# Second spectral piece behind the first W piece, gate_w row ahead of w_down, w_up in nine loads

## The chip, the cores and the metric

One NeuronCore of a Trainium2 chip runs the whole program. The metric is the device time of one execution in microseconds (us), lower is better. The profile is one execution, so a stage is read from it and a difference of a few us in the total is read from the timed runs.

## The reference, cut to what matters

Forward and all gradients of a gated mix of a spectral filter and a gated feed-forward block:

```python
g = sigmoid((x * gate_w).sum(-1, keepdims=True))     # x: 2048 x 576
a = irfft2(rfft2(x) * (w_r + 1j * w_i))              # spectral branch
b = (gelu(x @ w_gate) * (x @ w_up)) @ w_down         # w_gate, w_up: 576 x 4608
out = g * a + (1 - g) * b                            # returned with 7 gradients
```

## The kernel before: the parts that matter

Phase one walks 18 groups of the hidden dimension, each in four steps of 512 rows. A step on TensorE is: 16 z matmuls and four small ones, the xy matmuls in two halves, then "jobs" (weight-gradient work, here W: pieces of 16 matmuls of 1.75 us, and dwd pieces of 8 of 0.98 us), with a few spectral pieces between them. The scheduling is by program order, engine by engine.

```python
z, xy_full = H_mm(g, m)                   # TensorE; z is in pool pz, one buffer
...
second()                                  # second xy half, its q, xb, hu copies on ScalarE
jobs = carry + hs                         # (weight, function) pairs: W and dwd pieces
us = sum(j[0] for j in jobs)
at, k, late = 0.0, 0, [sigs]
for w, f in jobs:
    if k < n and at >= k * us / n:        # n spectral pieces, evenly spaced
        fft_next(); k += 1                # matmuls to pz (TensorE), copy out (ScalarE)
    f()                                   # W or dwd matmuls; every second one ends in a ScalarE copy
    at += w
    if late and at >= 2.5:
        late.pop()()                      # sigs: two sigmoids (ScalarE), then 8 VectorE operations
while k < n:
    fft_next(); k += 1
```

A spectral piece writes `pftile()`, which from the second group on is always the one buffer of `pz` that z uses too. So TensorE may start a piece, or the next z, only when the last piece has been copied out. The pieces come in three stretches: forward (f1, f2: lines L549, L566), middle (s2, s1: L659, L748) and inverse (Z, ZU, d: L794, L806, L820/L822).

Phase two reads the stored activations back, transposed (`pin`, six buffers), and multiplies them with `wgT`, `wd_all`, `wuT` in jobs called g, b, u.

```python
ensure()                                  # first six pin loads; all loads are in one queue (SP)
for f0 in range(0, NFC, FCB):
    LD.dma_start(wd_all[:, f0:f0 + FCB, :], ...)          # w_down, 5.2 MB in three
... # the last W pieces of phase one
gwr = p2res.tile([1, D], BF16, name="gwr")                # memory that phase one used
LD.dma_start(gwr[:], gate_w.rearrange("(o d) -> o d", o=1))
... # for job i: one w_up load of 6 blocks if i > 1; spread_gw() (needs gwr) at i == 1
```

## Time and profile before

| | us |
|---|---|
| median of the first 3 runs (range) | 1506.61 (1506.12 to 1510.05) |
| span of the profiled run | 1507.8 |
| TensorE busy | 1396.5 |
| ScalarE busy | 721.8 |
| VectorE busy | 731.7 |

With TensorE busy 93% of the span, only its idle time and its time at a lowered clock can be won. The lines that show where it waits are in the prediction below.

For comparing kernels I cut each span at the first matmul of certain steps (start times in the TensorE timeline, subtracted): "head" to the start of the second group; "forward" to step 11; "middle" to step 46; "inverse" to step 65 (steps counted from 0, four a group); "last steps" to phase two; "to first b" job; "b jobs" to the first u job; "rest".

| kernel | head | forward | middle | inverse | last steps | to first b | b jobs | rest |
|---|---|---|---|---|---|---|---|---|
| before | 92.9 | 105.0 | 463.0 | 289.5 | 111.8 | 33.8 | 75.2 | 336.6 |

### The profile page before, as it was taken

How to read it: one execution, taken by the hardware profiler on the slowest of the kernel's cores; microseconds unless marked ns; L12 is line 12 of the kernel's file. 1: busy time of each engine (PE TensorE's matmuls, PEld its weight loads, DVE VectorE, ACT ScalarE, POOL GpSimd, SP SyncE). 2: the span in 40 equal slices, each digit the busy share in tenths (PEclk: the TensorE clock that was granted, in tenths of full speed). 3: DMA queues.
4: the chain of work that ended last, by engine and by line, in shares of the span. 5: the costliest groups of instructions: out<-in, count | busy, mean ns of one | idle time of the engine just before them, and what ended most of it. 6: DMA issues, size and time to landing. Idle time of an engine off the chain costs nothing.

```text
span 1507.8 us, 28114 instructions
## 1 busy us (share of the span) xinstructions
PE 1396.5 (93%) x11342; PEld 1028.9 (68%) x11414; DVE 731.7 (49%) x1394; ACT 721.8 (48%) x1311; POOL 125.7 (8%) x230
## 2 busy tenths in 40 slices
PE   6888899999999999999998999999998999999997
PEld 4556566666666666766666666678676777777775
DVE  6674456777766776755555554553000461222110
ACT  5776677777777776666566666663000000000000
POOL 3000010011001001100101000000000110000000
PEclk9999999999999999999999999999999999999999
DMA  5333354544564453453444454576999998877773
GB/s 188 95 101 112 98 139 117 152 111 133 147 156 119 128 157 99 121 148 99 123 138 113 129 150 124 138 166 142 224 186 197 207 217 158 168 160 162 157 151 70
DMA packets 516381, 214.96 MB, mean 143 GB/s; under 512 B 312825, under 2 KB 510458, under 8 KB 516250
## 3 DMA queue, kind: packets, MB, share of 16 engines
q1 hardware_dynamic: 506618, 192.64, 54.7%
q0 software_dynamic: 7824, 19.49, 4.2%
q8 instruction: 89, 1.46, 0.4%
q10 hardware_dynamic: 1808, 1.02, 0.2%
q14 instruction: 42, 0.34, 0.1%
HBM read 40.76 MB, written 93.84 MB: 89 GB/s over the span
## 4 chain that ended last, share of the span: by engine, by line
PE 81%; ACT 10%; issue 3%; DVE 2%; DMA 2%; POOL 0%; ACTq 0%; DVEq 0%; POOLq 0%
PE acc L1094 27%; PE xy L392 16%; PE wps L495 15%; PE z L380 9%; PE wps L478 7%; ACT om L433 3%; PE xy L387 2%; PE z L383 2%; ACT dw L456 1%; ACT s L434 1%; PE wps L508 1%; DMA pin<-scr 1%; DMA gwr<-in_gate_w_dram 1%; ACT Xg L664 1%; ACT ZT L797 1%
## 5 line engine op out<-in xcount | busy, mean ns | idle before, releaser
L1094 PEld LDWEIGHTS <-pin 128*128 128x128 bf16 x3456 | 339.0, 98 | 92.0 <-DMA pin<-scr 5.0
L392 PE MATMUL xy<-wgu,xT 128*128 128x512 bf16 x1080 | 247.8, 379 | 10.2 <-issue 9.5
L495 PEld LDWEIGHTS <-xn 128*128 128x128 bf16 x2304 | 224.4, 98 | 29.2 <-issue 0.2
L392 PEld LDWEIGHTS <-xT 128*128 128x128 bf16 x1152 | 106.9, 98 | 149.3 <-issue 31.2
L380 PE MATMUL z<-wdT,dOT 128*128 128x256 bf16 x1152 | 145.7, 282 | 33.6 <-ACT Xg L664 14.2
L402 ACT ACTIVATE da<-z,omg 128x256 bf16<-128x256 f32 x288 | 113.0, 475 | 125.5 <-PE z L383 125.5
L1111 ACT COPY bo<-acc 128x288 f32<-128x288 f32 x32 | 12.8, 399 | 316.5 <-PE acc L1094 291.8
L380 PEld LDWEIGHTS <-dOT 128*128 128x128 bf16 x1152 | 115.8, 101 | 57.7 <-issue 40.4
L438 DVE TENSOR_TENSOR xb<-xb,s 128x1024 bf16<-128x1024 bf16 x72 | 49.8, 692 | 211.1 <-ACT s L434 211.1
L478 PE MATMUL wps<-dB,A 128*128 128x288 bf16 x1152 | 151.1, 286 | 0.0
L1094 PE MATMUL acc<-wd_all,pin 128*128 128x288 bf16 x1152 | 143.1, 286 | 4.1 <-DMA pin<-scr 4.1
L1094 PE MATMUL acc<-wgT,pin 128*128 128x288 bf16 x1152 | 146.6, 289 | 0.0
L1094 PE MATMUL acc<-wuT,pin 128*128 128x288 bf16 x1152 | 143.6, 286 | 0.0
L495 PE MATMUL wps<-dHu,xn 128*128 128x256 bf16 x1152 | 132.7, 272 | 0.0
L495 PE MATMUL wps<-dHg,xn 128*128 128x256 bf16 x1152 | 132.5, 273 | 0.0
L478 PEld LDWEIGHTS <-A 128*128 128x128 bf16 x1152 | 112.0, 98 | 28.3
L409 ACT ACTIVATE q<-xy 128x512 bf16<-128x512 f32 x144 | 86.1, 598 | 61.4 <-PE xy L392 61.4
L501 POOL DMA_DIRECT2D out_dram<-dw x67 | 48.8, 728 | 606.3 <-ACT dw L456 594.7
L1171 DVE SCALAR_TENSOR_TENSOR f32t<-gwf,dlog,b16t 128x576 f32<-128x576 f32 x16 | 13.1, 818 | 173.5 <-DMA b16t<-dxa_scr 173.5
L417 DVE TENSOR_SCALAR s<-q 128x1024 bf16<-128x1024 bf16 x72 | 30.7, 426 | 136.3 <-ACT q L409 136.3
L456 ACT CAST dw<-wps 128x512 bf16<-128x512 f32 x72 | 42.2, 586 | 93.5 <-PE wps L495 93.5
L412 ACT CAST hu<-xy 128x512 bf16<-128x512 f32 x144 | 86.9, 603 | 0.0
(197 smaller groups left out, 1637.5 us busy)
## 6 DMA issues: line engine op xcount, KB each, us to landing
scr<-A SPq DMA_DIRECT2D x72, 256.0 KB, 2.6
scr<-dHg SPq DMA_DIRECT2D x72, 256.0 KB, 2.9
scr<-dHu SPq DMA_DIRECT2D x72, 256.0 KB, 3.4
out_dram<-dw POOLq DMA_DIRECT2D x67, 128.0 KB, 2.2
wd_all<-in_B_w_down_dram SPq DMA_DIRECT2D x3, 1728.0 KB, 14.6
out_dram<-dwd POOLq DMA_DIRECT2D x34, 144.0 KB, 3.2
scr_p<-Vt SPq DMA_DIRECT2D x32, 145.0 KB, 3.0
wgu<-in_B_w_gate_dram SPq DMA_DIRECT2D x18, 256.0 KB, 3.3
```

The source lines that it names most:

```text
L380: nc.tensor.matmul(zo(t), lhsT=dOT[:, ci, t, :], rhs=wdT[:, ci, :], start=(t % 4 < 2 and ci == 0), stop=False)
L392: nc.tensor.matmul(xy[k][:, t % 2, :], lhsT=xT[:, ci, t, :], rhs=wgu[:, ci, :], start=False, stop=(ci == 3))
L402: nc.scalar.activation(da[:, t, :], z[:, t % 2, t // 2, :], ACT.Copy, scale=omg32[:, 4 * m + t:4 * m + t + 1])
L409: nc.scalar.activation(q[:, h, :], xy[:, :, 0:FG], ACT.Square)
L412: nc.scalar.copy(hu[:, h, :], xy[:, :, FG:2 * FG])
L433: nc.scalar.activation(om[:], s[:], ACT.Sigmoid, scale=-2.0 * C_GELU)
L438: V.tensor_tensor(xb[:], xb[:], s[:], op=ALU.mult)
L456: nc.scalar.copy(out, in_)
L478: nc.tensor.matmul(wps[:, :288], lhsT=tl(0, t)[:, fch * P:(fch + 1) * P], rhs=dB[:, t, h * 288:(h + 1) * 288], start=(t == 0), stop=(t == ...
L495: nc.tensor.matmul(wps[:, cc, :], lhsT=xn[:, t, (c0 + cc) * P:(c0 + cc + 1) * P], rhs=tl(k, t), start=(t == 0), stop=(t == T - 1))
L501: wst[0].dma_start(ov[:, c0:c0 + TPB, fsl], dw[:])
L1094: nc.tensor.matmul(acc[:, :288], lhsT=src[:, r, :], rhs=w_of(r)[:, h * 288:(h + 1) * 288], start=(first and r == 0), stop=(last and r == F ...
```

## The change

Its intent: the copy of a step's second spectral piece should no longer wait behind the sigmoids and a W copy on ScalarE, the gate_w row should not wait behind w_down, and w_up should load in smaller pieces spread over more jobs.

```diff
-                jobs = carry + hs
-                us = sum(j[0] for j in jobs)
                 at, k, late = 0.0, 0, [sigs]
-                for w, f in jobs:
-                    if k < n and at >= k * us / n:
+                for w, f in carry + hs:
+                    if k < n and at >= (0.0, 1.0, 3.6, 5.0)[k]:
                         fft_next()
                         k += 1
+                    if late and at >= 1.6 and k >= min(n, 2):
+                        late.pop()()
                     f()
                     at += w
-                    if late and at >= 2.5:
-                        late.pop()()
...
     wd_all = p2r.tile([P, NFC, D], BF16, name="wd_all")
+    gwr = p2r.tile([1, D], BF16, name="gwr")
+    LD.dma_start(gwr[:], gate_w.rearrange("(o d) -> o d", o=1))
...
-        LD.dma_start_transpose(wuT[k][:, r0:r0 + 6, :], B_w_up[:, f0 * P:(f0 + 6) * P])
+        LD.dma_start_transpose(wuT[k][:, r0:r0 + 4, :], B_w_up[:, f0 * P:(f0 + 4) * P])
...
-        wT_loads = [(k, r0) for k in range(NB) for r0 in (0, 6)]
+        wT_loads = [(k, r0) for k in range(NB) for r0 in (0, 4, 8)]
...
-        gwr = p2res.tile([1, D], BF16, name="gwr")
-        LD.dma_start(gwr[:], gate_w.rearrange("(o d) -> o d", o=1))
...
-            if i > 1 and wT_loads:
+            if i > 0 and wT_loads:
```

The first hunk holds two effects: the **place** of the second piece (behind one W or dwd piece, not at an even share of the work) and the **order** on ScalarE (sigmoids behind the second copy).

## The prediction

> **What bounds the kernel now.** I read the page first (busy shares, then the chain that ended last), then who waited for whom on TensorE stage by stage, then the timelines of single steps, last the windows for the granted clock.
>
> ```profile
> PE 1396.5 (93%) x11342; PEld 1028.9 (68%) x11414; DVE 731.7 (49%) x1394; ACT 721.8 (48%) x1311; POOL 125.7 (8%) x230
> ...
> PE 81%; ACT 10%; issue 3%; DVE 2%; DMA 2%; POOL 0%; ACTq 0%; DVEq 0%; POOLq 0%
> ```
>
> TensorE (PE) is the bound: 111 us of the 1507.8 us span are idle, and only those, and time at a lowered clock, can be won while its work stays the same. The order view of both kernels has 22830 TensorE instructions in each, so no matmul is removed. The waits of 195 to 680 us, then of 680 to 960 us:
>
> ```profile
> PE z L380 <- ACT Xg L664: 14.2, 8, 1.8
> PE z L380 <- ACT Vt L751: 9.7, 8, 1.2
> ...
> PE pf L820 <- ACT ZT L797: 7.0, 7, 2.2
> PE pf L794 <- ACT ev L826: 6.5, 5, 1.8
> PE pf L820 <- ACT ZU L809: 4.9, 3, 1.9
> PE pf L806 <- ACT ev L826: 3.5, 2, 1.8
> ```
>
> Columns: who waits, for what, us in total, times, longest. Every line is TensorE waiting for a ScalarE (ACT) copy of a spectral piece. The piece (pf) and the next step's z share one PSUM buffer, so nothing goes into it until the previous piece is copied out. Two stretches of ScalarE show why the copy is late or not:
>
> ```profile
> 405.69 1.28 ACT L664 CAST Xx<-pf 64x578 bf16<-64x578 f32 x2
> 407.86 0.59 ACT L456 CAST dw<-wps 128x512 bf16<-128x512 f32 x1 [0.88 <-PE wps L495]
> 408.34 1.06 ACT L433 ACTIVATE om<-s 128x1024 bf16<-128x1024 bf16 x1
> 409.43 1.06 ACT L434 ACTIVATE s<-s 128x1024 bf16<-128x1024 bf16 x1
> 410.39 1.27 ACT L664 CAST Xg<-pf 64x578 bf16<-64x578 f32 x2
> ...
> 432.96 0.85 ACT L751 CAST Vt<-pf 128x580 bf16<-128x580 f32 x1
> ```
>
> The second piece's copy (410.39) stands behind the W copy and two sigmoids, 2.5 us of work, and the next z waits 1.78 us for it. Phase two (from 1062 us):
>
> ```profile
> 1062.21 8.98 PE L1094 MATMUL acc<-wgT,pin 128*128 128x288 bf16 x72
> 1074.91 0.63 PE L1085 MATMUL acc<-gwr,onesr 1*128 1x288 bf16 x2 [3.71 <-DMA gwr<-in_gate_w_dram]
> 1075.47 20.65 PE L1094 MATMUL acc<-wgT,pin 128*128 128x288 bf16 x144
> 1095.96 35.44 PE L1094 MATMUL acc<-wd_all,pin 128*128 128x288 bf16 x288
> 1132.42 8.99 PE L1094 MATMUL acc<-wd_all,pin 128*128 128x288 bf16 x72 [1.01 <-DMA pin<-scr]
> 1143.25 8.99 PE L1094 MATMUL acc<-wd_all,pin 128*128 128x288 bf16 x72 [1.84 <-DMA pin<-scr]
> 1153.52 6.67 PE L1094 MATMUL acc<-wd_all,pin 128*128 128x288 bf16 x53 [1.28 <-DMA pin<-scr]
> ```
>
> A 1.1 KB row, queued behind 5.2 MB of w_down, costs 3.71 us; then 144 matmuls take 20.65 us where 288 take 35.44, so 17.7 at full pace; then three waits for transposed input sum to 4.1 us. The slow 144 have their reason in the windows, whose third-last column is the granted clock:
>
> ```profile
> 1076.00:1078.00 2.00, 2.00 (x10) 1.29 (x9) 0.16 (x1) 0.00 (x0) 0.00 (x0) 0.50 1.14 208
> 1082.00:1084.00 2.00, 2.00 (x19) 1.60 (x17) 0.00 (x0) 0.00 (x0) 0.00 (x0) 1.00 0.54 106
> ```
>
> **What the Trainium skill says.** "TensorE: Matmul & The Clock Gate", part 1 on the clock gate: after about one idle window of 3.4 us the array falls to half clock, and a busy window restores it; the window is free-running. The trace agrees in kind: 0.50 above, and half pace for some 3.4 us at 138, 155, 733, 795, 886 and 917 us, each after waits of 1.8 to 3 us. Here less idle than a full window is enough, and other waits of 1.8 us bring none, which suits a free-running window. The same page, on architectural detail: ScalarE and VectorE are strict FIFOs. The trace agrees: the copy at 410.39 starts as the second sigmoid drains, though its matmuls ended at 408.07. "DMA: Bandwidth & Descriptors", on latency and other measured facts, has 261 GB/s for a DMA transpose with a non-contiguous middle dimension. Here the stretch 1100 to 1150 us moves 164 to 204 GB/s at full DMA share, and that measurement is what I use.
>
> **The change, part by part.** Part one: in each of the 68 steps after the first group, a second piece now follows the first W half (16 matmuls, 1.75 us, or 8 dwd matmuls, 0.98 us), and its copy precedes the sigmoids. This removes the wait at the end of a step, but puts the second piece so close that TensorE waits for the first piece's copy. That copy cannot start before the q, xb, hu copies of the second xy half. Readiness after the last xy matmul, from the trace: for s2 pieces (L659) 3.1 us (matmuls to 403.91, copies to 406.97); for s1 (L748) 2.5 us (431.32 to 433.81; 2.4 in a shorter case); for Z 2.55, of which 0.37 is already seen as a wait at 788.50; for d 2.2; for ZU 1.9. TensorE's cover is the first piece (s1 and s2 0.25, Z 0.45, d 0.5, ZU 0.1) plus 1.75 or 0.98. So the new wait is 1.1 for s2 and 0.55 for s1 ahead of a W half; 1.9 and 1.15 ahead of a dwd half; 0.37, 0, 0 for Z, d, ZU ahead of W, and 1.1, 0.7, 0.8 ahead of dwd.
>
> Middle stretch (195 to 680 us). The order view gives 15 steps with s2 before W, 9 with s1 before W, 1 with s2 before dwd, 6 with s1 before dwd: 15 x 1.1 + 9 x 0.55 + 1.9 + 6 x 1.15 = 30.3 us new. Removed: 14.2 + 9.7 + 0.4 = 24.3. Loss 6.0 us.
>
> Inverse stretch (680 to 960 us, 19 steps with two to four pieces). Removed: 7.0 + 6.5 + 4.9 + 3.5 + 1.8 (ev, L820) + 1.0 (z for ZU) = 24.7. New, step by step: first-piece waits sum to 5.5 (5 Z before W at 0.37, then dwd steps 0.7, 0.7, 0.8, 1.1, and small remains); six steps now have their last piece directly ahead of z and wait for its whole copy (d and ZU about 0.8 each, Z 1.2 each), 5.5 together; third pieces waiting for a copy behind sigmoids and W copy, about 0.8. Sum 11.8, gain 12.9. No wait is over 1.3 us, so I expect the four half-clock spells here (733, 795, 886, 917) to go, all but about half of one: 3.5 x 3.4 us x 0.5 = 6 us.
>
> Forward stretch (123 to 211 us, six steps). Removed 11.4 (two waits of 3.0, 2.0, 1.8 and small ones). New 9.7: 0.5 and 0.6; then 3.4 and 2.4 where a third piece still sits behind the sigmoids; 1.5 and 1.4 around the table pieces. Gain 1.7. Its two half-clock spells stay.
>
> Part two, the gate_w row: ahead of all input loads it lands long before 1071 us; the ones row it multiplies is set at 1069.8, also in time. From 1071.2 to 1096.0 us TensorE would need 0.3 + 17.7 = 18.0 us instead of 24.8: gain 6.8, of which 3.7 is wait and about 3 clock.
>
> Part three, nine w_up loads of four blocks from the second job on, in place of six of six. Before, a job asks for three inputs (1.18 MB) and 0.88 MB of w_up in 8.85 us, 233 GB/s, more than the 164 to 204 moved. After, 1.18 + 0.59 MB, 200 GB/s, about what the queue does, and it starts where DMA is half idle (shares 0.46 to 0.83 at 1082 to 1090). With six input buffers ahead, nearly all of 4.1 us go; I take 3.7.
>
> Sum: +6.0 - 12.9 - 6.0 - 1.7 - 6.8 - 3.7 = -25.1; I give 2 us back for waits that I can't see, and come to 1506.6 - 23.1 = 1483.5 us.
>
> **The rivals.** One: the old waits simply go and nothing takes their place, since the PSUM buffer is free early enough. Then phase one wins 24.3 + 24.7 + 11.4 plus 10 of clock, and the time is about 1430. For it speaks the aim of the change; against it the 0.37 us already seen at 788.50 and the copies' end at 406.97, 1.1 us after a W half would be done. Two: the second copy delays the sigmoids, so VectorE becomes the bound. In steps with dwd the sigmoids end some 2 us later; VectorE's idle before the next step's first operation was as small as 0.63 us (445.54). But its chain of eight has a whole step of slack. If it does bind, 5 to 10 us are lost, about 1490. Three: w_up's first load, now ahead of inputs ten to twelve, starves the first b job as w_down still lands. That makes a wait of 2 to 4 us and perhaps another half-clock spell: 1488. Four: the middle stretch's new waits lower the clock, one spell costing 1.7 us; against it, its present 1.78 us waits never did.
>
> **Range and chances.** My unsure terms: clock spells +-5, middle +-4, inverse +-4, phase two +-4; together about +-9. Predicted 1483.5 us, range 1473 to 1493. Faster by over 2% means under 1476.5, some 7 us below: 0.2. Within 2%: 0.78. Slower by over 2%: 0.02.
>
> **What would show it.** Right: TensorE's waits for Xg at the next z vanish and waits of pieces L659 and L748 for the previous piece's copy appear, near 30 us together; the inverse stretch's waits halve, its clock is 1.00; the gate_w wait is gone and the 144 matmuls take 17.7 us; at most one input wait stays. Wrong: no wait inside the middle steps (rival one), VectorE idle near zero there (rival two), or an input wait at the first b job (rival three).

## The result, and the profile after

The changed kernel's median is 1481.82 us (4 runs, 1480.72 to 1484.17), that of the kernel before in the same rounds 1508.33. The ratio is 0.9825, 95% interval 0.9802 to 0.9848. Ratios here are the mean time of one kernel's runs over that of the other's of the same rounds, so not quite the ratio of the medians. By 1508.33 x 0.0175 that is 26.4 us, under 2%, for which the prediction gave 0.78.

| kernel | head | forward | middle | inverse | last steps | to first b | b jobs | rest |
|---|---|---|---|---|---|---|---|---|
| before | 92.9 | 105.0 | 463.0 | 289.5 | 111.8 | 33.8 | 75.2 | 336.6 |
| changed | 96.5 | 99.2 | 468.8 | 269.0 | 111.8 | 26.9 | 72.7 | 334.0 |

The page of the changed kernel:

```profile
PE 1391.3 (94%) x11342; PEld 1024.0 (69%) x11414; DVE 732.4 (50%) x1394; ACT 722.1 (49%) x1311; POOL 125.7 (8%) x230
```

The same matmuls, 5.2 us less busy, so the difference lies in how long they took. Who TensorE waits for in the changed kernel's middle stretch (waiter, releaser, us in total, times, longest):

```profile
PE pf L659 <- ACT Xx L664: 7.6, 8, 1.0
PE pf L659 <- ACT Vt L751: 6.8, 6, 1.1
PE pf L748 <- ACT Xg L664: 6.7, 7, 1.0
...
PE pf L748 <- ACT Vt L751: 3.4, 9, 0.4
PE pf L659 <- DMA Vp<-scr_x: 2.7, 1, 2.7
```

No z (L380) waits for a copy here any more; instead each second piece but one waits for the first piece's copy, 24.5 us in 30 waits against 24.3 us in 18 before. The last line is the remaining one: it waits for a transfer. A step of it, on TensorE and then on ScalarE:

```profile
418.76 0.41 PE L659 MATMUL pf<-Vp,Btab 128*128 128x289 bf16 x2
419.01 1.91 PE L495 MATMUL wps<-dHg,xn 128*128 128x256 bf16 x16
421.87 0.41 PE L748 MATMUL pf<-qm,BTtab 128*128 128x290 bf16 x2 [0.95 <-ACT Xg L664]
422.12 1.91 PE L495 MATMUL wps<-dHg,xn 128*128 128x256 bf16 x16
423.87 3.66 PE L495 MATMUL wps<-dHu,xn 128*128 128x256 bf16 x32
```

```profile
420.54 1.28 ACT L664 CAST Xg<-pf 64x578 bf16<-64x578 f32 x2
422.32 0.82 ACT L751 CAST Vt<-pf 128x580 bf16<-128x580 f32 x1 [0.50 <-PE pf L748]
422.99 1.05 ACT L433 ACTIVATE om<-s 128x1024 bf16<-128x1024 bf16 x1
424.08 1.06 ACT L434 ACTIVATE s<-s 128x1024 bf16<-128x1024 bf16 x1
425.04 0.57 ACT L456 CAST dw<-wps 128x512 bf16<-128x512 f32 x1
```

The second copy (422.32) is now ahead of the sigmoids, as intended. But the first copy ends at 421.82 while the one W piece was done by about 420.76 (419.01 + 1.75). Note what the idle column leaves out: from 419.01 to 421.87 are 2.86 us where an undisturbed piece takes 1.75 (422.12 to 423.87), so the wait costs 1.11 us, and the column says 0.95.

The waits of the changed kernel's inverse stretch:

```profile
...
PE pf L820 <- ACT ZT L797: 2.6, 5, 1.1
PE z L380 <- ACT ZT L797: 2.2, 2, 1.1
PE z L380 <- ACT ev L826: 2.2, 3, 0.7
PE pf L820 <- ACT ZU L809: 0.8, 1, 0.8
PE pf L794 <- ACT ev L826: 0.7, 1, 0.7
PE pf L806 <- ACT ev L826: 0.7, 1, 0.7
...
```

With two lines of 0.5 and 0.4 that is 10.1 us, against 24.7 before. The clock followed. Two windows in which the kernel before fell to half clock for a while (third column from the end is the granted clock), and one of them in the changed kernel:

```profile
730.00:740.00 10.00, 7.67 (x64) 4.83 (x60) 6.06 (x10) 5.28 (x9) 1.77 (x3) 0.83 0.35 95
880.00:890.00 10.00, 8.12 (x62) 6.31 (x60) 6.36 (x12) 4.70 (x8) 0.72 (x1) 0.84 0.24 74
```

```profile
730.00:740.00 10.00, 9.84 (x92) 6.47 (x91) 6.22 (x11) 7.20 (x13) 1.77 (x3) 1.00 0.45 122
```

Of all 10 us windows from 90 to 1180 us none of the changed kernel is under 1.00. Phase two of the changed kernel, to be held against the lines in the prediction:

```profile
1054.22 0.41 PE L1083 MATMUL acc<-gwr,onesr 1*128 1x288 bf16 x2
1054.57 17.81 PE L1092 MATMUL acc<-wgT,pin 128*128 128x288 bf16 x144
1072.22 53.09 PE L1092 MATMUL acc<-wd_all,pin 128*128 128x288 bf16 x432
1126.21 8.99 PE L1092 MATMUL acc<-wd_all,pin 128*128 128x288 bf16 x72 [0.90 <-DMA pin<-scr]
1135.61 8.99 PE L1092 MATMUL acc<-wd_all,pin 128*128 128x288 bf16 x72 [0.40 <-DMA pin<-scr]
```

The row is there in time, the 144 matmuls take 17.81 us, and three input waits of 1.6 us together (the third, 0.30, is not shown) are left of 4.1.

### The profile page after: what moved, and what is told of

Same layout as the page of the kernel before. It is cut to its first block, busy times and chain, and to the rows that moved or that the text cites. A ratio compares the mean times of both kernels' runs of the same rounds, so it can differ in the third digit from the quotient of the medians.

```text
span 1478.9 us, 28110 instructions
## 1 busy us (share of the span) xinstructions
PE 1391.3 (94%) x11342; PEld 1024.0 (69%) x11414; DVE 732.4 (50%) x1394; ACT 722.1 (49%) x1311; POOL 125.7 (8%) x230
## 4 chain that ended last, share of the span: by engine, by line
PE 80%; ACT 10%; DVE 4%; issue 3%; DMA 1%; SPq 0%; POOL 0%; ACTq 0%; DVEq 0%; POOLq 0%
PE acc L1092 28%; PE xy L392 15%; PE wps L495 12%; PE wps L478 8%; PE z L380 8%; PE wps L508 2%; PE xy L387 2%; ACT hu L412 2%; ACT xb L411 2%; PE z L383 1%; ACT q L409 1%; ACT Vt L751 1%; ACT om L433 1%; ACT Xx L664 1%; ACT Xg L664 1%
## 5 line engine op out<-in xcount | busy, mean ns | idle before, releaser
L1109 ACT COPY bo<-acc 128x288 f32<-128x288 f32 x32 | 12.7, 398 | 306.8 <-PE acc L1092 282.2
L380 PE MATMUL z<-wdT,dOT 128*128 128x256 bf16 x1152 | 140.6, 276 | 13.5 <-ACT Y L556 5.2
L495 PE MATMUL wps<-dHg,xn 128*128 128x256 bf16 x1152 | 136.2, 272 | 0.0
L380 PEld LDWEIGHTS <-dOT 128*128 128x128 bf16 x1152 | 112.9, 99 | 33.5 <-issue 18.3
L411 ACT CAST xb<-xy 128x512 bf16<-128x512 f32 x144 | 83.6, 580 | 0.0
```

The lines of the kernel that those rows point to most:

```text
L380: nc.tensor.matmul(zo(t), lhsT=dOT[:, ci, t, :], rhs=wdT[:, ci, :], start=(t % 4 < 2 and ci == 0), stop=False)
L411: nc.scalar.copy(xb[:, h, :], xy[:, :, 0:FG])
L495: nc.tensor.matmul(wps[:, cc, :], lhsT=xn[:, t, (c0 + cc) * P:(c0 + cc + 1) * P], rhs=tl(k, t), start=(t == 0), stop=(t == T - 1))
```

## The experiments

All gave correct results. Ratios are to the kernel before in the same rounds. Twelve runs were made, two of them of the unchanged kernel for its profile alone; their stages are in one table at the end of this section.

### The three parts one by one

**p_row**: the kernel before with only the gwr hunks of the diff.

> The kernel before with the gate_w row alone moved ahead. My theory (wait plus half-clock spell): the 3.7 us wait goes and the 144 matmuls after it take 17.7 us in place of 20.65, so 6.8 us less up to the first b job; in all 4 to 7 us less (about 1501), since the three input waits may grow as TensorE now meets w_up's loads earlier. Rival (only the wait counts, the clock falls anyway): 3.7 us less and the 144 matmuls stay near 20 us.

Ratio 0.9983 (0.9969 to 0.9998), 1504.13 us. In its profile the stretch to the first b job fell from 33.8 to 27.4, with the 144 matmuls at 17.81 us: wait and clock both went, as my theory says. The three input waits stayed (1.04, 1.58, 1.40). But the timed gain, 2.6 us, is smaller than the profile's 6.4. Hence the repeats below.

**p_wup**: only the w_up hunks.

> The kernel before with w_up in nine loads from the second job alone. My theory (transfers outrun the queue): the three input waits of 4.1 us fall under 1 us together, 3 to 4 us less, about 1503. Rival (the first load, now earlier, starves the first b job while w_down still lands): a new input wait of 2 to 4 us near the first b job and no gain.

Ratio 0.9988 (0.9974 to 1.0001), 1504.85 us: too little to tell from nothing by time. In the profile no input wait is left, b jobs take 70.6 in place of 75.2 us, and the row still costs a wait of 4.63 us. No wait at the first b job, so the rival falls. Other profiles warn against reading much into one: p_fill, with the old six loads, has only 0.92 us of input waits, and s_first, with nine, has 2.70.

**p_steps**: only the first hunk.

> The kernel before with the new order of the steps alone. My theory: forward and inverse stretch gain (about 5 and 20 us with their half-clock spells, as the trace of the changed kernel shows), the middle stretch loses 4 to 6; about 18 us less, 1488, and phase two as in the kernel before. Rival (parts don't add, since phase two's start depends on the steps): over 22 or under 14 us less.

Ratio 0.9838 (0.9823 to 0.9854), 1482.73 us: 24 us of the 26. It beat my 18 us, and reached the rival's mark: the parts do not simply add. Forward, inverse and last steps are those of the changed kernel to 0.1 us; the middle stretch is 1.4 us longer, since here a half-clock spell (granted clock 0.83 from 228 to 238 us) followed the wait for the transfer. The surplus is in phase two, where the row, still loaded behind w_down, cost only this:

```profile
1056.37 0.40 PE L1083 MATMUL acc<-gwr,onesr 1*128 1x288 bf16 x2 [0.70 <-DMA gwr<-in_gate_w_dram]
```

A candidate cause: in the last group, where no spectral pieces are left, the new rule emits the sigmoids after one W piece instead of two. The last stores then leave the queue earlier, and so do the input loads behind them. They started 23.7 us ahead of phase two (1023.00 to 1046.68), before 21.5 (1040.67 to 1062.21).

**b_last** tests that alone:

```diff
-                    if late and at >= 2.5:
+                    if late and at >= (1.6 if g == NG - 1 else 2.5):
```

> The kernel before with the sigmoids of the last group's four steps emitted after 1.6 instead of 2.5 us of W work (there are no spectral pieces left in them). My theory (the steps' part already heals the row's wait, since the last stores, and with them the input, w_down and row loads behind them in the same queue, start earlier): first input load about 2 us earlier relative to phase two (23.5 in place of 21.5 us ahead of it), the row's wait under 1.5 us and the stretch to the first b job 27 to 30 us in place of 33.8; 2 to 6 us less in that profile. Rival (the loads' start has nothing to do with it): the input loads start at 21.5 us and the stretch stays at 33 us or more.

The input loads started 23.7 us ahead of phase two (1043.71 to 1067.38), the row's wait was 1.30 us, the stretch to the first b job 28.3 us, all as expected by my theory. Ratio 0.9977 (0.9954 to 0.9999), 1504.58 us. So the step part by itself heals most of the row's wait, and little is left there for the row part. (The row's matmul starts 12.7 us after phase two begins in the first profile, 9.7 in p_steps, 10.3 in b_last.)

### How much of phase two is the one profile

**b_again**, **b_again2**: the kernel before, unchanged.

> The kernel before once more, unchanged, for its profile. My theory (the steps are the same to a few tenths in every execution, while the prologue and phase two vary): stages from the second step to phase two within 1 us of the first profile, but the stretch from phase two to the first b job, 33.8 us there, anywhere from 28 to 34 as the row lands earlier or later. Rival (phase two repeats too): 33 to 35 us.

> As the run before it, a second profile of the unchanged kernel before, with the same expectations of both theories.

1503.68 and 1505.24 us (single runs, their state unknown). Forward to last steps repeat to 0.1 us. To the first b job: 31.8 and 31.6 us, with row waits of 3.19 and 2.96. Phase two as a whole took 439.7 and 440.0 us, against 445.6 in the first profile. So the profile that I predicted from had some 5.7 us in phase two that the two repeats do not have, and its head was at the short end of the 92.8 to 98.0 us seen in all profiles. My theory held: phase two varies while the steps do not, though the first stretch stayed in the upper half of 28 to 34. The rival's 33 to 35 falls. Which profile is typical stays open: p_wup, whose row is loaded in the same old place, has 34.2 us there, and the two repeats ran below the 1510.03 us median of the same kernel's eleven timed runs of that session (1501.64 to 1514.55).

### Is it the clock that makes 144 matmuls slow?

**p_fill**: the kernel before with useless matmuls during the row's wait.

```diff
             if i == 1:
+                ps = acc_pair()[0]
+                for r in range(34):
+                    nc.tensor.matmul(ps[:, :288], lhsT=wgT_all[0][:, 0:P], rhs=wgT_all[0][:, 0:288], start=True, stop=True)
                 spread_gw()
```

> The kernel before, the row still late, with 34 matmuls that nobody reads put ahead of the row's matmul, to keep TensorE busy through the wait. My theory: the wait of 3.7 us is replaced by 4.1 us of useless work, but no half clock follows, so the 144 matmuls after it take about 17.7 us in place of 20.65 and the time up to the first b job falls by about 2.5 us; in all 0 to 2.5 us less. Rival (the slow matmuls come from the inputs' transfers, not from the clock): the 144 stay at 20 us or more, and the time grows by 0.4 us.

Its TensorE timeline:

```profile
1075.03 4.33 PE L1204 MATMUL acc<-wgT 128*128 128x288 bf16 x34
1079.29 0.41 PE L1085 MATMUL acc<-gwr,onesr 1*128 1x288 bf16 x2
1079.63 17.81 PE L1094 MATMUL acc<-wgT,pin 128*128 128x288 bf16 x144
```

The row's load was issued 0.9 us ahead of phase two (1065.33 to 1066.20), no earlier than the 1.1 us of the first profile, and the inputs' transfers were the same, yet the 144 matmuls ran at full pace: 17.81 us. So the slow pace followed from TensorE's idleness. The time, ratio 0.9992 (0.9978 to 1.0005), does not tell 1 us from nothing, since the filler takes what the clock gives back.

### Place and order of the second piece

**m_old**: the changed kernel with the old rule in the middle stretch.

```diff
+                old = 11 <= pr < 46
-                    if k < n and at >= (0.0, 1.0, 3.6, 5.0)[k]:
+                    if k < n and at >= (k * us / n if old else (0.0, 1.0, 3.6, 5.0)[k]):
...
-                    if late and at >= 1.6 and k >= min(n, 2):
+                    if not old and late and at >= 1.6 and k >= min(n, 2):
...
+                    if old and late and at >= 2.5:
+                        late.pop()()
```

> The changed kernel with the old order in the middle stretch alone. My theory: 3 to 6 us faster than the changed kernel, about 1477, with waits for Xg and Vt at the next z back at 24 us and those at L659 and L748 gone. Rival (the middle stretch lost nothing but a single late transfer): under 3 us faster or no faster.

Ratio 0.9764 (0.9737 to 0.9791), 1471.12 us. The middle stretch is back at 463.0 us, 5.8 less than the changed kernel's, and the waits at z are back at 14.2 and 9.7. The median is 10.7 us under the changed kernel's, more than I expected. They were not run in the same rounds; of the 9.0 us between the two profiles the middle stretch has 5.8, the shorter head 2.1 and the b jobs 1.7, less 0.6 elsewhere. The rest I leave as spread between rounds.

**m_late**: the changed kernel, but in the middle stretch with the second piece behind two W pieces (or three dwd pieces), its copy still ahead of the sigmoids.

```diff
-                    if k < n and at >= (0.0, 1.0, 3.6, 5.0)[k]:
+                    if k < n and at >= (0.0, 2.6 if 11 <= pr < 46 else 1.0, 3.6, 5.0)[k]:
```

> The changed kernel, but in the middle stretch the second piece behind two W halves (three of dwd) in place of one, its copy still ahead of the sigmoids. My theory (the new waits come from the first piece's copy, ready 2.4 to 3.1 us after the last xy matmul): two halves cover 3.2 to 3.75 us, so the waits for the previous piece's copy, 27 us in all in the changed kernel's middle stretch, go but for under 1 us, and none comes at the next z: 24 to 27 us less than the changed kernel, about 1456. Rival (VectorE binds once the sigmoids come late, here a further 1 us later): less than 12 us gained and new waits of ScalarE or TensorE for VectorE.

Ratio 0.9637 (0.9611 to 0.9662), 1452.59 us. The middle stretch is 441.3 us, 27.5 less than the changed kernel's. The waits on TensorE from 195 to 680 us (the inverse stretch begins at 638):

```profile
...
PE pf L659 <- DMA Vp<-scr_x: 2.6, 1, 2.6
PE pf L820 <- ACT ZT L797: 0.7, 2, 0.4
PE z L380 <- ACT ev L826: 0.7, 1, 0.7
...
```

Every wait for an s1 or s2 copy is gone, at the start and at the end of a step. One step of it on ScalarE, whose sigmoids come later than in either kernel relative to the step:

```profile
396.67 1.28 ACT L664 CAST Xx<-pf 64x578 bf16<-64x578 f32 x2
398.83 0.59 ACT L456 CAST dw<-wps 128x512 bf16<-128x512 f32 x1 [0.88 <-PE wps L495]
399.31 1.29 ACT L664 CAST Xg<-pf 64x578 bf16<-64x578 f32 x2
400.50 1.06 ACT L433 ACTIVATE om<-s 128x1024 bf16<-128x1024 bf16 x1
```

TensorE waits for VectorE nowhere in that stretch, and ScalarE's own copies and sigmoids follow each other without a gap for it in this step. VectorE itself idles 116 us from 195 to 680 us waiting for the sigmoids. So the rival that late sigmoids make VectorE the bound falls.

**s_first**: the new place, but the sigmoids ahead of the second piece.

```diff
                 for w, f in carry + hs:
+                    if late and k >= 1 and at >= 1.0:
+                        late.pop()()
...
-                    if late and at >= 1.6 and k >= min(n, 2):
-                        late.pop()()
```

> The changed kernel with the pieces at their new places, but the sigmoids ahead of the second piece's copy. My theory: in steps with three or four pieces the third piece, and in those with two the next z, rarely waits more than in the changed kernel, as the sigmoids now start as soon as the first piece's copy is out, 2.5 us after the last xy matmul, and copy two ends near 6 us; so the place alone gives most of the inverse stretch's gain: within 6 us of the changed kernel, about 1484. Rival (the order is what counts): the waits of the kernel before return, over 1495.

Ratio 0.9851 (0.9826 to 0.9876), 1484.22 us, as expected. The inverse stretch is 268.6 us, no worse than the changed kernel's 269.0. So the new order was not needed there: the early place alone does it. The middle stretch is 472.3 us, 9.3 more than before.

**o_only**: the new order, the old places.

```diff
-                for w, f in carry + hs:
-                    if k < n and at >= (0.0, 1.0, 3.6, 5.0)[k]:
+                jobs = carry + hs
+                us = sum(j[0] for j in jobs)
+                for w, f in jobs:
+                    if k < n and at >= k * us / n:
```

> The changed kernel with the pieces at their old places in every step, but the sigmoids behind the second piece's copy. My theory (place and order are two effects, order does the good, the near place does the harm): the middle stretch as in m_late, without waits, about 25 us less than the changed kernel there; the inverse stretch, where a third piece is evenly spaced, about as the changed kernel's or up to 8 us worse; in all about 1460. Rival (it is the early place that wins): slower than the changed kernel.

Ratio 0.9616 (0.9589 to 0.9642), 1450.76 us, better than I expected: the middle stretch is m_late's 441.3 us, and the inverse stretch 266.5, better than with the new places. Its waits on TensorE from 195 to 636 us, but for 4.4 us of "issue", are one line:

```profile
PE pf L659 <- DMA Vp<-scr_x: 2.8, 1, 2.8
```

With the kernel before and s_first all four combinations are measured. Middle stretch: 463.0 us with neither, 472.3 with the early place, 441.3 with the order, 468.8 with both. Inverse stretch: 289.5, 268.6, 266.5, 269.0. So the order alone does all the good; the early place does that of the inverse stretch too, but adds nothing to the order and costs the middle stretch 27.5 us.

**best**: o_only with the loads for the second block of the spectral weights issued two pieces earlier. The wait for `Vp<-scr_x`, 2.7 us in the changed kernel and 2.8 in o_only, happens once, for a load that a spectral piece issues into the same queue as the stores, which wait for VectorE.

```diff
                     side.extend(products(p))
-                    if p == 0:
-                        prefetch(p + 1)
+                if which == "x" and j == 1 and p == 0:
+                    prefetch(p + 1)
```

> The kernel with the pieces at their old places and the sigmoids behind the second copy (1450.8 us), with the second block's spectral loads issued two pieces earlier. My theory: the single wait of 2.8 us for that transfer goes and nothing else changes, 1448 us. Rival (the loads then hold up the stores or weight loads behind them in the queue): the wait moves to another transfer and the time stays at 1450 to 1452.

1444.35 us (5 runs, 1442.54 to 1446.90), ratio 0.9579 (0.9557 to 0.9600): 4.2% under the kernel before, and 2.5% under the changed kernel's median (other rounds). The wait is gone, and no other took its place. The middle stretch is 4.2 us shorter, more than the 2.8 of the wait: in o_only a half-clock spell followed it (granted clock 0.83 from 228 to 238 us), in best none (1.00).

### The stages of all kernels

One profile each, us:

| kernel | head | forward | middle | inverse | last steps | to first b | b jobs | rest |
|---|---|---|---|---|---|---|---|---|
| b_again | 92.8 | 105.0 | 463.0 | 289.5 | 111.8 | 31.8 | 72.7 | 335.2 |
| b_again2 | 94.2 | 105.0 | 463.0 | 289.5 | 111.8 | 31.6 | 73.0 | 335.4 |
| p_row | 94.2 | 105.0 | 463.0 | 289.5 | 111.9 | 27.4 | 75.1 | 335.0 |
| p_wup | 94.3 | 105.0 | 463.0 | 289.5 | 111.8 | 34.2 | 70.6 | 335.1 |
| p_fill | 95.9 | 106.0 | 463.0 | 289.4 | 111.8 | 31.1 | 71.7 | 336.5 |
| b_last | 98.0 | 105.0 | 463.0 | 289.4 | 111.9 | 28.3 | 74.5 | 335.6 |
| p_steps | 96.5 | 99.2 | 470.2 | 269.0 | 111.8 | 27.7 | 73.4 | 334.6 |
| m_old | 94.3 | 99.2 | 463.0 | 269.0 | 111.9 | 27.2 | 71.0 | 334.3 |
| s_first | 94.3 | 98.3 | 472.3 | 268.6 | 112.6 | 27.2 | 74.1 | 335.5 |
| m_late | 96.0 | 100.8 | 441.3 | 269.0 | 111.8 | 27.9 | 70.6 | 334.4 |
| o_only | 95.9 | 99.0 | 441.3 | 266.5 | 111.8 | 27.0 | 72.3 | 335.3 |
| best | 95.6 | 97.7 | 437.1 | 266.5 | 111.8 | 28.2 | 70.5 | 334.8 |

## Why the prediction was right, and where it was not

1483.5 us was predicted, 1481.82 measured. Step by step:

- **Middle stretch, a loss of 6.0: right**, 5.8 measured. That the first piece's copy is the new limit is shown: with two W pieces as cover (m_late) its waits vanish. Single waits were near the sizes predicted: 1.11 us against 1.1 for s2 ahead of W in the step shown above. (For s1 the prediction's own figures give 0.50 and 1.27, where it adds 0.55 and 1.15; that moves its sum by 0.3 us. Its forward terms add up to 9.8, not 9.7.) Two terms were off and nearly cancelled. The yardstick is best, whose middle stretch (437.1 us) has neither these waits nor a half-clock spell: against it the old waits cost 25.9 us (24.3 predicted, from the idle column) and the new ones 31.7 (30.3 predicted). The step with s2 ahead of dwd (1.9 predicted) waits 2.7 us for a transfer that I did not foresee.
- **Inverse stretch, a gain of 18.9 with its clock: right**, 20.5 measured. Waits fell by 14.6 (12.9 predicted), and all four half-clock spells went, not three and a half. They stood in all seven profiles with the old step rule, at the same steps, and in none of the other seven. That this needs the new order was only my reading: s_first has the gain without it.
- **Forward stretch, a gain of 1.7: too small**, 5.8 measured. The step that failed is "Its two half-clock spells stay". In the kernel before, its windows at 130 and 150 us had a clock of 0.96 and 0.83; the changed kernel's have 1.00, although a wait of 1.89 us and one of 0.83 follow each other closely. That is in part luck: m_late has the same two waits and one spell (clock 0.83 from 136 to 146 us), and its forward stretch takes 100.8 in place of 99.2 us. The waits fell by 2.9, not 1.7. (The prediction also gives this stretch's times late: by the cut used here it runs from 92.9 to 197.9 us.)
- **Row, 6.8: right in that one profile** (33.8 to 26.9), too large for timed runs. Against the two repeats of the kernel before the stretch gains 4.8, the row alone gave 2.6 by time (95% interval 0.3 to 4.7), and with the new step order only 0.8 (27.7 to 26.9) was left for the row and the earlier w_up loads together. The unstated assumption that failed is that the load's timing in phase two is the same in every execution and independent of part one; b_last shows the dependence.
- **Nine loads, 3.7: too large.** 2.5 in the profile (75.2 to 72.7), of which the repeats of the kernel before (72.7 and 73.0) leave nearly nothing. Alone (p_wup) they did remove every input wait in its one profile. Over all profiles the b jobs take 73.7 us on average in the seven with six loads (71.7 to 75.2) and 71.7 in the seven with nine (70.5 to 74.1). So about 2 us is likelier; p_wup's 1.8 us by time is not clear of nothing.
- **The allowance of 2 us** was right in size only, and that the total fits is in part luck, since the errors above cancel. Against the first profile the stages gain 32.4 us after the head, which is 3.6 longer: 28.8 in all. Against the mean of the two repeats the changed kernel gained 5.8 forward, lost 5.8 in the middle, gained 20.5 in the inverse stretch and 6.2 in phase two (439.85 to 433.6), 26.7 together, next to 26.4 by time.

Of the rivals, the first (waits simply go, 1430) falls: 24.5 us of new copy waits took the place of 24.3. The second (VectorE binds) falls by m_late. The third (w_up starves the first b job) did not show in the changed kernel or in p_wup; o_only's longest input wait is 0.88 us, 45 us after its first b job began. The fourth (clock spells in the middle) did not come in the changed kernel's profile, but in p_steps, whose steps are the same, one followed the wait for the transfer; the copy waits brought none.

## What to carry to other kernels

With one shared PSUM buffer, ask of each piece two times: when the copy ahead of it can be finished, and when its own copy can start on a FIFO engine behind everything emitted earlier. Moving a piece earlier only shifts the wait if its predecessor's copy is not yet out; reordering the copy engine, with enough TensorE work between two pieces, removes it on both sides. Before adding up gains in a stretch bound by transfers, take the profile of the unchanged kernel twice more: there a single one had 5.7 us that others had not, while the stages bound by engines repeated to 0.1 us in the kernel before. Where a wait brings a half-clock spell in one profile and none in the next, as in p_steps and the changed kernel, these differ too, here by 1.4 us.

## What the Trainium skill lacked or had wrong

- "TensorE: Matmul & The Clock Gate", part 1, has the array fall to half clock after at least one idle window of about 3.4 us. Here spells followed single waits as short as 1.76 us (the one that ends at 916.15 us in the kernel before; granted clock 0.83 from 914 to 924 us), while sixteen waits of 1.2 to 1.8 us in its middle stretch brought none. One wait of 2.7 us at the same step brought a spell in p_steps and none in the changed kernel. Filling the idle time with useless matmuls (p_fill) kept the pace: 17.81 us in place of 20.65 for 144 matmuls.
- "DMA: Bandwidth & Descriptors", latency and other measured facts, has 261 GB/s for a transpose whose middle dimension is not contiguous. The stretch of 1100 to 1150 us here, in which all loads issued are transposes of two kinds (13 of `pin`, 5 of `wuT`), moved 164 to 204 GB/s at full DMA share. Whether they are of the page's kind is not shown.
